# A gated linear attention block and a SiLU feed-forward block on one core: output and state products moved next to the scores of the following chunk

## The chip, the cores and the metric

The kernel runs on one core of one Trainium2 chip. The metric is the device time of one execution in microseconds. The median of three executions of the kernel before is 556.96 us (556.51 to 557.35).

## The reference

The first block is a recurrent linear attention with a gate for each row of the state (4 batches, 8 heads, 768 tokens, head width 48). The second multiplies the 3072 rows of its output by `w_in` (384 x 2048), applies `h * sigmoid(h)`, and multiplies by `w_out` (2048 x 384). q, k, v and alpha are float32, the weights arrive as float64.

```python
for t in range(S):
    state = alpha[:, :, t, :, None] * state + einsum('bhd,bhe->bhde', k[:, :, t], v[:, :, t])
    y[:, :, t] = einsum('bhd,bhde->bhe', q[:, :, t], state)
x = y.transpose(0, 2, 1, 3).reshape(B * S, H * D)
h = x @ w_in
g = h * (1.0 / (1.0 + np.exp(-h)))
return g @ w_out
```

## The kernel before

**Chunks and steps.** The sequence is cut into six chunks of 128 tokens; with four batches this makes NT = 24 chunks of work, n = 0 to 23, where n and n + 4 belong to the same batch. An outer loop over `step` has four quarters (called slots in the code). In each quarter it issues one or two attention stages, and then `fill` issues pieces of the feed-forward block. The stages of chunk n are:

- `products(n)`, in step n, quarter 1: VectorE brings alpha into a transposed layout (32 x 32 block transposes), takes a backward running product of it (a scan, u), the smallest values (`least`), transposes k and forms kp = k * u.
- `quotient(n)`, step n, quarter 2: VectorE takes a reciprocal and a forward scan p, transposes q, and writes p = q * p. The first matmul of the scores waits for this last write.
- `flip(n)`, step n, quarter 3: VectorE transposes kp and a DMA carries it out and back (`land`) to get it in the layout that the states need (kn).
- `scores(n)`, step n + 1, quarter 0: 16 small matmuls of kp and p into two PSUM tiles named ps_a; ScalarE copies them to g, GpSimd masks them; ScalarE scales the state of the batch.
- `values(n)` gives y: 16 matmuls of g with v and 12 of the state with p into a ps_a tile, which ScalarE copies to xt, the input of the feed-forward block. `states(n)` then makes 16 matmuls of kn and v into one more ps_a tile, and VectorE adds them to the state (two additions, `st`). Both stand in step n + 1, quarter 3. From chunk 20 on there is no states stage.

There are three ps_a buffers of one PSUM bank each. Chunks 0 to 7 (NA = 8) use TensorE transposes in place of VectorE's, and `settle` after them frees the memory of the weight conversion and loads the first chunk of the second kind.

**The feed-forward block.** Four chunks make a group (GB = 4, six groups). Groups 0 and 1 use plain products with `w_in` (`enter_plain`): a piece is six matmuls of 128 x 256. Groups 2 to 5 use a fast matrix multiplication with 20 products in place of more (`enter`, seven pieces for each pair of column blocks). It needs sums of blocks of `w_in` (`sums_w`, 23 for each pair, 128 x 256 each, on VectorE) and sums of blocks of x (`sums_x`, 11 for a group, named xc). The product with `w_out` is a Strassen-like scheme (`leave`, seven pieces for each half of a group; a piece is eight matmuls of 128 x 192 into one of two PSUM banks named ps_o). Pieces 1, 3 and 4 of a `leave` end with two subtractions each on cells of g (`subtract`, in place; a subtraction has to wait until TensorE has read those cells), pieces 3, 5, 6 and 7 end with a store of a 128 x 192 block to the output. `side_by_side` is an addition of two cells of g that follows the SiLU of the last piece.

**Order.** `fill` paces the pieces: `marks` gives, for each phase of pieces, the quarter by which it has to be done, and a piece that needs y of a chunk is not issued before `values` of that chunk (`bridged`). From chunk 8 on, TensorE's instructions stay in program order; VectorE's, ScalarE's and the queues' are put in order by the compiler's scheduler where a line does not call `keep_in_program_order`. On the chip each engine works its list off in that order, so an instruction that waits holds up all that stand behind it on its engine. `audit` adds reductions over the inputs on VectorE that decide at the end whether the fast path was valid (a flag, read before the last pieces).

Around step 10 the order of TensorE's work in the kernel before is as follows (P a piece of `enter_plain`, L.k piece k of `leave(0, 1)`, y and S values and states, sc scores):

```text
sc8  P P P  y8 S8  L.1  sc9  P L.2  P L.3  y9 S9  P  sc10  L.4  P L.5  P  y10 S10  L.6  sc11  P L.7  P P  y11 S11
```

Of the kernel before, what the change touches and what calls it, by code (L numbers as in the profile page):

```python
# [13 lines left out]
ALU = mybir.AluOpType  # L14
# [341 lines left out]
def quotients(  # L356
# [20 lines left out]
    dve, act, gps = nc.vector, nc.scalar, nc.gpsimd  # L377
# [17 lines left out]
    C = 128  # L395
# [39 lines left out]
    def ps_attn(n=C):  # L435
        return ps_a.tile([128, 512], F32, name="ps_a").rearrange("p (j c) -> p j c", c=n)
# [152 lines left out]
    def sums_w(pair, upto):  # L589

        r = slice(2 * pair, 2 * pair + 2)
        while sums_done[pair] < min(upto, len(SUMS_W)):
            to, sa, a, sb, b = SUMS_W[sums_done[pair]]
            tc.keep_in_program_order(
                combine(block_w(to)[:, r], sa, block_w(a)[:, r], sb, block_w(b)[:, r]))
            sums_done[pair] += 1
# [108 lines left out]

    def turned(x, to):
        x = x[:, 32:].rearrange("p (g j d) -> p g j d", j=4, d=D)
        dve.transpose(to.rearrange("p g (b j) -> p g j b", j=4), x[:, :, :, 0:32])

    def products(n):  # L710

        c = ctxs[n]
        sg = seg[0 if late else n % 2]
        ps = {}

        for name in ("a", "k", "q"):
            if n >= NA:
                if name == "a":
                    turned(c[name], tokens(sg))
                    load(n + 1, "a")  # L720
                continue
            if n < GB and name != "a":

                at = "kq".index(name)
                ps[name] = (bank(at) if n == 1 else out_bank(at, 512)).rearrange("p (j c) -> p j c", c=C)
            else:
                ps[name] = ps_attn()
            for j in range(NP):
                pe.transpose(ps[name][:, j, :], c[name][:, 2 * j : 2 * j + 2, :], ident)
            if name == "a":  # L730
                act.copy(tokens(sg), ps[name])  # L731
        end = NP * W
        u = upool.tile([128, end + 1], F32, name="u")
        dve.tensor_tensor_scan(u[:, end - 1 :: -1], sg[:, end:0:-1], one[:, end:0:-1],  # L734
                               0.0, ALU.mult, ALU.add)

        dve.tensor_single_scalar(least[:, n, :], u[:, 0:end:W], 2.0**-64, ALU.max)
        kp = c["kp"] = turns(kps, n) if n < NA else kps[0]
        ut = tokens(u)
        if n >= NA:  # L740
            ps["k"] = late["turn"].tile([128, NP, C], F32, name="turn")
            turned(c["k"], ps["k"])
            load(n + 1, "k")
        if n < NA:
            dve.tensor_tensor(kp, ps["k"], ut, ALU.mult)
            quotient(n, sg, ps["q"])
            return
        j = NP // 2
        dve.tensor_tensor(kp[:, 0:j], ps["k"][:, 0:j], ut[:, 0:j], ALU.mult)
        k, ut = [x[:, j:].rearrange("p j (e c) -> p j e c", e=2) for x in (ps["k"], ut)]  # L750
        dve.tensor_tensor(kp[:, j:].rearrange("p j (e c) -> p j e c", e=2)[:, :, ::-1], k, ut, ALU.mult)
        c["sg"] = sg
# [90 lines left out]
    def values(n):  # L843
# [17 lines left out]
        if e == 0:  # L861
            xts[half] = xtp.tile([128, NKT, TB], F32, name="xt")
        act.copy(xts[half][:, :, e * C : (e + 1) * C], py[:, 0:NKT])  # L863
    def states(n):
        c = ctxs.pop(n)
        ci, b, vn = c["ci"], c["b"], c["v"]
        if ci < NCH - 1:

            ps = ps_attn()
            for j in range(NP):  # L870
                for i in range(4):
                    r = slice(32 * i, 32 * i + 32)
                    kn = c["kn"][:, j, r] if n < NA else c["kn"][:, i, 32 * j : 32 * j + 32]
                    pe.matmul(ps[r, j, 0:D], lhsT=kn, rhs=vn[:, 2 * j + i // 2, 0:D],
                              start=True, stop=True)
            for u in range(2):
                r = slice(64 * u, 64 * u + D)
                s, x = st[b][r, :, u, :], ps[r, :, 0:D]
                if ci > 0:
                    dve.tensor_tensor(s, x, s, ALU.add)  # L880
                else:
                    act.copy(s, x)
# [28 lines left out]
    def enter_plain(grp, h, pair):  # L911

        if h == 0:
            g_tiles(grp, pair)
        xt = xts[2 * grp + h]
        for f in range(8 * pair, 8 * pair + 8, 2):
            ps = bank(f // 2 % 3).rearrange("p (e n) -> p e n", e=2)
            for e in range(2):
                for t in range(NKT):
                    pe.matmul(ps[:, e, :], lhsT=w_in[:, t, (f + e) * 128 : (f + e + 1) * 128],  # L920
                              rhs=xt[:, t, :], start=(t == 0), stop=(t == NKT - 1))
            q, i = divmod(f, 4)
            act.activation(gts[grp, h, pair][:, i : i + 2, q % 2, :], ps, AF.Silu)  # L923
            if grp == 1 and pair == h == 0:
                differences(f // 2)
                differences(4 + f // 2)
            if grp > 0 and f % 8 == 6:
                side_by_side(grp, h, pair)
            yield

    def enter(grp, pair):
# [92 lines left out]
    def cells(grp, h, pair, m, k):  # L1024

        return gts[grp, h, pair][:, k::2, :, m * C : (m + 1) * C]
# [3 lines left out]
    def side_by_side(grp, h, pair):  # L1030

        x = cells(grp, h, pair, 1, 0)
        dve.tensor_tensor(x, x, cells(grp, h, pair, 1, 1), ALU.add)

    def leave(grp, h):

# [26 lines left out]

        def done():
            if 2 * grp + h in (1, 2):
                sums_w(2 * grp + h - 1, 4 * next(steps) + 4)

        def new(i):
            return out_bank(i, HO)
# [54 lines left out]
    def group(grp):  # L1124
        return [[(enter(grp, pair), 12, GB * grp + GB)] * 7 for pair in range(2)]

    def output(grp):
        return [[(leave(grp, h), 12, GB * grp + GB)] * 7 for h in range(2)]

    def both(x, y):  # L1130
        for i in range(max(len(x), len(y))):
# [3 lines left out]
    for h in range(2):  # L1135
        for pair in range(2):
            pieces += [plain(0, h, pair)] * 4
    pieces += [plain(1, 0, 0)] * 4 + [(leave(0, 0), 12, GB)] * 7
    phases = [len(pieces)]
    pieces += [plain(1, 1, 0)] * 4  # L1140
    both([(leave(0, 1), 12, GB)] * 7, [plain(1, 0, 1)] * 4 + [plain(1, 1, 1)] * 4)
    phases.append(len(pieces))
    before = output(1)
    for grp in range(2, NG):
# [12 lines left out]

    def go_on():

        nonlocal done  # L1160
        next(pieces[done][0], None)
        done += 1

    audits = audit()
    done, bridged = 0, 0
    STEPS = NT + 1
    SLOTS = 4

    marks = [2 * SLOTS + 2] + [(GB * i + 2 * GB) * SLOTS + 3 for i in range(len(phases))]

    def settle():

        first.close()
        late.update(look=pool("look"), part=pool("part"), turn=pool("turn"),
                    xc=pool("xc").tile([128, len(SUMS_X), TB], F32, name="xc"),
                    wx=pool("wx").tile([128, 8, NQ, 128], F32, name="wx"))
        quads = pool("quads")
        late["p"] = pool("p").tile([128, NP * W + 1], F32, name="p")
        late["quads"] = {name: quads.tile([128, 32 + 4 * NP * D], F32, name=f"{name}t") for name in "akq"}
        for name, t in late["quads"].items():  # L1180
            gps.memset(t, 1.0 if name == "a" else 0.0)
        load(NA)

    def fill(step, slot):

# [16 lines left out]

    for step in range(STEPS):
        if step == 1:
            load(NIN)
        stages = [[(scores, 1)], [(products, 0)], [(values, 1)], [(states, 1)]]
        if step == 1:

            stages = stages[1::-1] + stages[2:]
        elif step >= NA:  # L1210
            stages = [[(land, 1), (scores, 1)], [(products, 0)], [(quotient, 0)],
                      [(values, 1), (states, 1), (flip, 0)]]
        for slot, group in enumerate(stages):
            for stage, lag in group:
                n = step - lag
                if not 0 <= n < NT:
                    continue
                stage(n)
                if stage is values:
                    bridged = n + 1  # L1220
                if stage is states and n + 1 + NIN < NA:
                    load(n + 1 + NIN)
                if stage is states and n + NV < NT:
                    load_v(n + NV)
            if step * SLOTS + slot == (NA + 1) * SLOTS - 1:
                x = decayed.rearrange("p (o i c) -> p o i c", o=2, c=C)
                for r, o in later:
                    gps.memset(x[r, o, :, 0:CH], 0.0)
            fill(step, slot)
            if step * SLOTS + slot >= NA * SLOTS - 1 and conv_done[1] == NFT and not late:  # L1230
                settle()
# [82 lines left out]
```

## Time and profile before

| | |
|---|---|
| median of three executions | 556.96 us |
| the profiled execution | 557.26 us, of which the span from the first to the last instruction is 555.5 us |
| granted TensorE clock | 0.999 |
| TensorE matmul busy (PE) | 541.4 us, 97% of the span |
| weight loads busy (PEld) | 489.7 us, 88% |
| VectorE busy (DVE) | 445.4 us, 80% |
| ScalarE busy (ACT) | 208.5 us, 38% |
| GpSimd busy (POOL) | 76.1 us, 14% |
| DMA | 70.09 MB, mean 126 GB/s |

PE is TensorE's matmuls, PEld its weight loads, DVE VectorE, ACT ScalarE, POOL GpSimd, SPq the DMA queue of SyncE. An fp32 matmul appears as two instructions in the trace, so that a piece of six matmuls shows as x12 and a piece of eight as x16. The end of a matmul is modelled; where exact times matter, starts are compared. In a timeline row the first number is the start in us, the second the time that the row covers, and the bracket at the end gives the idle time before it and what ended it. In the view of waits, the numbers are the us in total, how many times, and the longest.

### The profile page before, as it was taken

The page shows a single profiled execution, that of the slowest core. Times are in us where ns is not written, and L with a number is a line of the kernel's source. Part 1 is how long each engine was busy: PE and PEld are TensorE (multiplying, and loading weights), DVE is VectorE, ACT ScalarE, POOL GpSimd, SP SyncE. Part 2 cuts the span into 40 slices and gives each one's busy share as a digit, 9 for nine tenths or more (in the row PEclk, how much of TensorE's full clock was granted, in tenths as well). Part 3 has the DMA queues.
Part 4 walks back from the last instruction along what each step waited for, and adds up shares of the span by engine and source line. Part 5 has one row for each costly group of instructions (what it writes and reads, how often), then busy time and mean ns, then how long its engine had stood idle before and what let it go on. Part 6 is the DMA issues. An engine that isn't in the chain of part 4 may idle for free. (4 is left out here: it accounts for less than half of the span.)

```text
span 555.5 us, 12640 instructions
## 1 busy us (share of the span) xinstructions
PE 541.4 (97%) x5026; PEld 489.7 (88%) x5026; DVE 445.4 (80%) x801; ACT 208.5 (38%) x466; POOL 76.1 (14%) x146
## 2 busy tenths in 40 slices
PE   6999999999999999999999999999999999999996
PEld 4788887998899999899999999988998999999996
DVE  5897788974999899997998986998884796945431
ACT  2556653223333253353353353344263342332100
POOL 3210000222210212021011021021121000001000
PEclk9999999999999999999999999999999999999999
DMA  9998971164454625355545654617642135500000
GB/s 215 246 249 210 232 195 33 47 161 116 117 136 125 159 63 138 86 145 149 139 112 139 193 139 120 191 27 183 170 137 91 54 91 169 172 11 22 10 24 30
DMA packets 99217, 70.09 MB, mean 126 GB/s; under 512 B 56272, under 2 KB 88656, under 8 KB 99152
## 3 DMA queue, kind: packets, MB, share of 16 engines
q1 hardware_dynamic: 97232, 65.30, 45.1%
q0 software_dynamic: 1920, 3.93, 2.0%
q8 instruction: 40, 0.66, 0.5%
q14 instruction: 25, 0.20, 0.1%
HBM read 61.34 MB, written 7.86 MB: 125 GB/s over the span
## 5 line engine op out<-in xcount | busy, mean ns | idle before, releaser
L388 PE MATMUL ps_o<-w_out,g 128*128 128x192 f32 x768 | 134.0, 328 | 0.5 <-DVE o L1056 0.5
L388 PEld LDWEIGHTS ps_o<-w_out,g 128*128 128x128 f32 x768 | 125.6, 190 | 3.5 <-DVE o L1056 1.0
L388 PE MATMUL ps_m<-xt,w_in 128*128 128x256 f32 x480 | 113.6, 383 | 1.5 <-ACT xt L863 1.1
L388 PEld LDWEIGHTS ps_m<-xt,w_in 128*128 128x128 f32 x480 | 89.1, 190 | 14.4 <-ACT xt L863 1.6
L388 PE MATMUL ps_o<-wt,g 128*128 128x192 f32 x576 | 99.7, 326 | 0.0
L388 PEld LDWEIGHTS ps_o<-wt,g 128*128 128x128 f32 x576 | 95.1, 190 | 1.6 <-issue 0.2
L388 PE MATMUL ps_m<-xc,w_in 128*128 128x256 f32 x288 | 70.7, 382 | 0.0
L388 PEld LDWEIGHTS ps_m<-xc,w_in 128*128 128x128 f32 x288 | 53.7, 190 | 7.0 <-DVE g L958 0.3
L1047 DVE TENSOR_TENSOR g<-g 128x512 f32<-128x512 f32 x72 | 50.1, 709 | 8.3 <-PE ps_o L388 8.3
L955 ACT ACTIVATE g<-g 128x1024 f32<-128x1024 f32 x32 | 33.1, 1056 | 61.2 <-DVE g L958 61.1
L1059 POOL DMA_DIRECT2D out_dram<-o x40 | 22.0, 551 | 219.5 <-DVE o L1056 113.7
L825 POOL TENSOR_SCALAR_AFFINE_SELECT g<-g 64x256 f32<-64x256 f32 x64 | 34.9, 546 | 124.4 <-ACT g L818 105.7
L388 PE MATMUL ps_m<-xc,wx 128*128 128x256 f32 x192 | 50.1, 383 | 1.0 <-DVE xc L586 1.0
L950 ACT COPY g<-ps_m 128x512 f32<-128x512 f32 x64 | 36.6, 588 | 37.0 <-PE ps_m L388 36.9
L388 PEld LDWEIGHTS ps_m<-xc,wx 128*128 128x128 f32 x192 | 35.2, 190 | 5.2 <-ACT u L1078 1.2
L958 DVE TENSOR_TENSOR g<-ps_m,g 128x512 f32<-128x512 f32 x56 | 37.1, 683 | 3.2 <-PE ps_m L388 2.7
L734 DVE TENSOR_TENSOR_SCAN u<-al,one 128x516 f32<-128x516 f32 x24 | 29.8, 1240 | 11.9 <-ACT al L731 11.6
L923 ACT ACTIVATE g<-ps_m 128x512 f32<-128x512 f32 x32 | 19.1, 597 | 41.7 <-PE ps_m L388 41.4
L950 ACT COPY part<-ps_m 128x512 f32<-128x512 f32 x32 | 18.9, 590 | 38.0 <-PE ps_m L388 24.0
L697 DVE TENSOR_REDUCE seen<-bits 128x1 f32<-128x512 int32 (+1 forms) x33 | 26.3, 823 | 5.7 <-DMA bits<-in_moe_w_in_dram 5.7
L764 DVE TENSOR_TENSOR_SCAN p<-al,inv 128x516 f32<-128x516 f32 x24 | 29.9, 1247 | 1.0 <-PE ps_a L388 0.3
L1056 DVE TENSOR_TENSOR o<-ps_o,u 128x192 f32<-128x192 f32 x24 | 8.5, 355 | 25.7 <-PE ps_o L388 22.8
(129 smaller groups left out, 648.5 us busy)
## 6 DMA issues: line engine op xcount, KB each, us to landing
bits<-in_moe_w_in_dram SPq DMA_DIRECT2D x24, 512.0 KB, 4.7
bits<-in_moe_w_out_dram SPq DMA_DIRECT2D x16, 384.0 KB, 3.9
at<-in_alpha_dram SPq DMA_DIRECT2D x64, 96.0 KB, 2.5
kt<-in_k_dram SPq DMA_DIRECT2D x64, 96.0 KB, 2.6
qt<-in_q_dram SPq DMA_DIRECT2D x64, 96.0 KB, 2.7
bits<-in_alpha_dram SPq DMA_DIRECT2D x9, 512.0 KB, 4.0
out_dram<-o POOLq DMA_DIRECT2D x40, 96.0 KB, 2.4
flips<-turn SPq DMA_DIRECT2D x12, 256.0 KB, 2.4
```

The source lines that it names most:

```text
L388: in_order(nc.tensor.matmul(*args, **kw))
L697: dve.tensor_reduce(seen[kind][which][:, i : i + 1], x, axis=AX, op=op, apply_absolute_value=True))
L734: dve.tensor_tensor_scan(u[:, end - 1 :: -1], sg[:, end:0:-1], one[:, end:0:-1], 0.0, ALU.mult, ALU.add)
L764: dve.tensor_tensor_scan(p[:, 0:end], sg[:, 0:end], iv[:, 0:end], 0.0, ALU.mult, ALU.add)
L825: gps.affine_select(x, x, pattern=[[0, NP], [1, CH]], compare_op=ALU.is_ge, fill=0.0, base=0, channel_multiplier=-1)
L923: act.activation(gts[grp, h, pair][:, i : i + 2, q % 2, :], ps, AF.Silu)
L950: act.copy(to, ps)
L955: act.activation(x, x, AF.Silu)
L958: dve.tensor_tensor(to, a, b, op)
L1047: dve.tensor_tensor(cells(grp, h, pair, *to), cells(grp, h, pair, *x), cells(grp, h, pair, *y), ALU.subtract)
L1056: dve.tensor_tensor(o, x, y, ALU.add)
L1059: (gps if grp < NG - 1 else nc.sync).dma_start(out[r : r + C, c * HO : (c + 1) * HO], o)
```

## The change

Seven edits, all of them in where work is issued; the number of matmuls, of VectorE operations and of bytes stays the same.

1. From step 9 on (chunks 8 to 23), `values(n)` and `states(n)` move from step n + 1, quarter 3, to step n + 2, quarter 0, directly ahead of `scores(n + 1)`. One more step is run (STEPS = NT + 2).
2. `states` then writes into a ps_o bank that the running `leave` does not hold at that moment (`left` counts its pieces) and no longer into a ps_a tile. When the next `leave` piece is the second or the fifth, that piece is issued first.
3. The end of each phase of pieces but the first is two quarters later (`marks`).
4. In `enter_plain` of group 1, the `side_by_side` addition is issued one piece later (`owed`).
5. Eight of the 23 sums of `w_in` for pair 0 are issued with the four pieces of `plain(1, 1, 0)`, and eight for pair 1 with the last two pieces of `leave(0, 1)`; both were issued later.
6. `settle` loads alpha of chunk 8 first, then v, then k and q; v of chunk 8 was loaded before in the quarter after `states(6)`.
7. A few instructions are pinned to program order (the first k transposes of chunk 9, an addition of g).

```diff
-            turned(c["k"], ps["k"])
+            turn_k = turned(c["k"], ps["k"])
+            if n == NA + 1:
+                tc.keep_in_program_order(turn_k)
...
-    def states(n):
+    def states(n, behind=False):
...
-            ps = ps_attn()
+            if behind:
+                ps = out_bank(0 if left in (3, 4, 5) else 1, 512).rearrange("p (j c) -> p j c", c=C)
+            else:
+                ps = ps_attn()
...
+            if grp == h == 1 and pair == 0:
+                sums_w(0, f + 2)
             if grp > 0 and f % 8 == 6:
-                side_by_side(grp, h, pair)
+                owed.append((done, grp, h, pair))
...
-        dve.tensor_tensor(x, x, cells(grp, h, pair, 1, 1), ALU.add)
+        add = dve.tensor_tensor(x, x, cells(grp, h, pair, 1, 1), ALU.add)
+        if grp == h == 1:
+            tc.keep_in_program_order(add)
...
         def done():
             if 2 * grp + h in (1, 2):
-                sums_w(2 * grp + h - 1, 4 * next(steps) + 4)
+                n = 4 * next(steps) + 4
+                sums_w(2 * grp + h - 1, n)
+                if grp == 0:
+                    sums_w(1, n - 20)
...
-        nonlocal done
+        nonlocal done, left
+        if pieces[done][0] in leaves:
+            left = left % 7 + 1
         next(pieces[done][0], None)
+        while owed and owed[0][0] < done:
+            side_by_side(*owed.pop(0)[1:])
         done += 1
...
-    STEPS = NT + 1
+    STEPS = NT + 2
...
-    marks = [2 * SLOTS + 2] + [(GB * i + 2 * GB) * SLOTS + 3 for i in range(len(phases))]
+    marks = [2 * SLOTS + 2] + [(GB * i + 2 * GB) * SLOTS + 3 + 2 * (i > 0) for i in range(len(phases))]
...
-        load(NA)
+        load(NA, "a")
+        load_v(NA)
+        load(NA, "kq")
...
-            stages = [[(land, 1), (scores, 1)], [(products, 0)], [(quotient, 0)],
-                      [(values, 1), (states, 1), (flip, 0)]]
+            lag = 2 if step > NA else 1
+            y = [(values, lag), (states, lag)]
+            stages = [[(land, 1), (scores, 1)], [(products, 0)], [(quotient, 0)], [(flip, 0)]]
+            stages[0 if lag == 2 else 3][0:0] = y
...
+                if stage is values and lag == 2 and left in (1, 4) and pieces[done][0] in leaves:
+                    go_on()
-                stage(n)
+                if stage is states:
+                    states(n, lag == 2)
+                else:
+                    stage(n)
...
-                if stage is states and n + NV < NT:
+                if stage is states and n + NV < NT and n + NV != NA:
                     load_v(n + NV)
```

Around step 10 TensorE's work in the changed kernel stands in this order:

```text
sc8  P P P  L.1  y8 S8 sc9  P L.2  P L.3  y9 S9 sc10  P L.4  P L.5  y10 S10 sc11  P L.6  P L.7  y11 S11 sc12
```

## The prediction

> **What bounds the kernel now.** I read the page first, then the view of waits of TensorE, then the timeline around each wait, and last the order in which VectorE's instructions stand in the built programs.
>
> ```profile
> PE 541.4 (97%) x5026; PEld 489.7 (88%) x5026; DVE 445.4 (80%) x801; ACT 208.5 (38%) x466; POOL 76.1 (14%) x146
> ...
> DVE  5897788974999899997998986998884796945431
> ```
>
> PE is busy all the time, so a microsecond in which it waits is a microsecond of the total; VectorE is nearly full in the middle slices too. What is left to gain is in PE's waits from step 10 on:
>
> ```profile
> PE ps_m L388 <- DVE xc L586: 1.0, 1, 1.0
> ...
> PE ps_a L388 <- DVE p L770: 0.5, 1, 0.5
> PE ps_m L388 <- DVE g L958: 0.4, 1, 0.4
> ```
>
> By the starts of matmuls these three cost 2.5 us: 1.13 at 367.1, 0.64 at 143.0 and 0.72 around 228. A fourth of that size, for the store `o` at 531.5, lies in the tail and stays.
>
> The third view is what a score block waits for. These are the timelines of TensorE and of VectorE around y of chunk 10 (columns: start, us, engine, line, operation):
>
> ```profile
> 168.76 2.75 PE L388 MATMUL ps_m<-xt,w_in 128*128 128x256 f32 x12
> 171.44 1.08 PE L388 MATMUL ps_a<-g,vn 128*32 128x128 f32 x32
> 172.34 0.84 PE L388 MATMUL ps_a<-p,st 128*32 128x128 f32 x24
> 173.00 0.52 PE L388 MATMUL ps_a<-vn,kn 128*32 128x48 f32 x32
> 173.45 2.87 PE L388 MATMUL ps_o<-w_out,g 128*128 128x192 f32 x16
> 176.25 0.90 PE L388 MATMUL ps_a<-p,kp 48*64 48x128 f32 x32
> ```
>
> ```profile
> 169.57 0.35 DVE L1056 TENSOR_TENSOR o<-ps_o,u 128x192 f32<-128x192 f32 x1
> 169.84 0.41 DVE L587 SCALAR_TENSOR_TENSOR w_in<-wx,w_in 128x256 f32<-128x256 f32 x1
> 170.17 0.88 DVE L582 TENSOR_TENSOR w_in<-wx,w_in 128x256 f32<-128x256 f32 x2
> 170.97 0.42 DVE L584 TENSOR_TENSOR w_in<-w_in 128x256 f32<-128x256 f32 x1
> 171.30 1.22 DVE L708 STREAM_TRANSPOSE turn<-kt 128x512 f32<-128x512 f32 x1
> 172.56 0.43 DVE L749 TENSOR_TENSOR kp<-turn,u 128x256 f32<-128x256 f32 x1
> 172.90 0.42 DVE L751 TENSOR_TENSOR kp<-turn,u 128x256 f32<-128x256 f32 x1
> 173.36 1.11 DVE L708 STREAM_TRANSPOSE turn<-qt 128x512 f32<-128x512 f32 x1
> 174.50 0.69 DVE L770 TENSOR_TENSOR p<-turn,p 128x512 f32<-128x512 f32 x1
> ```
>
> The store `o` empties the bank of L.5, which PE left at 168.76. The k and q transposes and p of chunk 11 stand behind it on VectorE's list, 5.6 us from 169.57 to 175.19. PE does not notice: between L.5 and the scores at 176.25 it has a plain piece (2.7 to the next start), y and states (171.44 to 173.45, 2.0) and L.6 (2.8).
>
> **The change part by part.** The sum is made against the profiled execution, 557.26 us, which stands 0.3 us above the median of 556.96.
>
> *Visits to the small matmuls.* y, states and scores are one visit in place of two, 15 times (y of chunks 8 to 22). What a visit costs PE besides its matmuls: the first piece behind it takes 0.11 longer (2.87 for the x16 at 173.45, 2.76 for the one at 518.64 below); on the way in, the last wide matmul starts 0.31 before the first small one (159.72 to 160.03) where wide ones follow each other by 0.22, 0.09 more; and the first wide one after the states starts some 0.11 late. A merged visit saves at most these 0.31, and nothing if the turn from states to scores costs as much. The nearest row, a score block that follows states directly at 17.77, starts 0.21 behind the last of them; I take 0.16, 15 x 0.16 = 2.4 us, ends 0 and 4.6. [...]
>
> *Scores of steps 10 to 13.* Here the change costs. With four pieces in a step in place of five, a `leave` piece now stands directly ahead of y, and the scores directly behind the states. From the end of that piece to the scores PE has 0.1 + 2.0 = 2.1 us of work. VectorE's list in the changed program keeps the subtraction or the store of that very piece in front of the k transpose:
>
> ```text
> step 10 (chunk  9): sub(L.1) kt kp kp w w qt sub(L.1) p
> step 11 (chunk 10): sub(L.3) kt sub(L.3) kp kp w qt w p
> step 12 (chunk 11): o(L.5) w w w w kt kp kp qt p
> step 13 (chunk 12): o(L.7) w w kt w kp kp w qt xc p
> ```
>
> (sub a subtraction of 512 columns, w a sum of w_in.) As steps between starts in the timeline: sub 0.60, kt 1.06, the two kp 0.80, qt 1.05, w 0.34, o 0.27, p whole 0.69. A subtraction starts when PE has read half the piece:
>
> ```profile
> 518.64 2.76 PE L388 MATMUL ps_o<-w_out,g 128*128 128x192 f32 x16
> ...
> 520.14 0.69 DVE L1047 TENSOR_TENSOR g<-g 128x512 f32<-128x512 f32 x1 [0.61 <-PE ps_o L388]
> ```
>
> 1.5 us after its start, with PE's way to the scores then 2.6 + 2.1 = 4.7. Step 10: 1.5 + 5.5 - 4.7 = 2.3 us of wait. Step 11: 1.5 + 5.6 - 4.7 = 2.4. Step 12: the rows above give the same ten operations as 5.6; with 0.2 from PE's end to the store, 5.8 - 2.1 = 3.7, and by the steps between starts 3.4; I take 3.5. Step 13: two more small sums and one store step instead of the longer sum, 5.7 + 0.2 - 2.1 = 3.8. Together 12.0, where before there were 0.6. VectorE is idle ahead of each of these pieces (about 8 us of work per step against PE's 11), so each wait starts anew and they add; ends 10 and 14. Deferring `side_by_side` does remove VectorE's 7.6 us wait for a SiLU, but the subtraction of L.1 then waits at the same place, to 139.9 where the sum was at 139.21.
>
> *Later steps.* With seven pieces in a step, the scores have cover. What is late next is xc, whose last nine sums now come behind the group's last two products. For group 4 VectorE has, from the product before them to the xc sum that the second entry piece reads, 37 operations: 14 x 0.60, 8 sums 2.9, alpha's chain 3.9, two transposes 2.1, two kp 0.8, two reductions 1.2, two stores 0.6, state additions 0.7, together 20.6. PE has 1.7 + 2.1 + 1.0 + 2.6 + 1.7 + 2.6 + 2.6 + 2.6 = 16.9. Wait 3.8; the same count before gives 1.2 where the trace shows 1.13. Likewise groups 3 and 5 give 0.7 and 0.3, and the first piece of `leave(3, 1)`, whose bank is emptied behind the chain of chunk 23, 1.5. Together 6.3; I take 6, ends 2 and 8. The 2.5 us of before are replaced by these.
>
> *What costs nothing, and why.* States in the ps_o bank wait for its store: ScalarE's copy after L.3 ends 0.4 after PE, VectorE's after L.5 1.0 in this phase and 2.7 at most, ahead of 2.0 us of y; uncovered it costs 0.7 once. L.2 reuses the bank of states 8: the state additions that free it end 2.7 after p on VectorE's list, PE has the scores and a plain piece of 3.6 in that time; without it, up to 2.7. v's loads go out a quarter later, behind flip on SP's queue and waiting there for the states, with kn and the next alpha behind them; all are used a step or two on, 14 us or more against the 2.7 that q's loads take to land. Alpha first at `settle` only reorders SP. The masks on POOL, with the output stores behind them, get a quarter more; ScalarE's copies of y and scores come in a row of 3 us, and the plain pieces have three banks. The 16 earlier sums (0.34 each) fill VectorE's idle stretch after 131.6 or stand in the lists above; without that they cost 5.4.
>
> Sum: 557.3 - 2.4 + 12.0 + 6 - 2.5 = 570.4 in the profile, 570 as a median.
>
> **The rivals.**
>
> *Only the scores wait.* The late xc is worked off while VectorE gains from PE's four waits. For it: VectorE at 250 to 260 has 31% free. Against: the waits of group 4 start from a place 170 us later. 557.3 - 2.4 + 12.0 + 0.5 - 2.5 = 564.9, median 564.6.
>
> *Faster.* One mechanism: VectorE reaches the k transposes before the `leave` piece ends, so that p is ready when the states are. Then the saved visits and the removed waits stand: 557.3 - 2.4 - 2.5 = 552.4. For it: kt of chunk 9 is fetched at 121 and transposed at 139.8, so the data would be there. Against: VectorE runs its list in order, and 5.6 us of it hang on a piece that ends 2.1 us ahead of the scores. It decides if all new waits together stay under 4.9 us.
>
> *No change.* Waits near 4.9 us, which needs the lists above to be wrong by half.
>
> **How the numbers follow.** Scores and later waits 0.72 (566 to 575); only the scores 0.16 (562 to 566); faster 0.07; no change 0.02; more than 575 by waits that I did not count 0.03. Predicted 570. All low costs together with the largest saving give 557.3 - 4.6 + 10 + 2 - 2.5 = 562.2, all high ones 576.8; the range is 562 to 575, which leaves about 1 in 8 out. About 0.2% is what a measurement of this kernel can tell from no change. Slower 0.72 + 0.16 + 0.03 = 0.91, same 0.02, faster 0.07.
>
> **What would show it.** PE's waits would have ps_a waiting for p four times or more, 10 us or more in total, at the first four merged visits after 140 us, each with VectorE idle shortly before, waiting for ps_o. xc would have 3 us or more near group 4's entry. The pieces behind merged visits would be as long as behind single ones, and 15 fewer. Wrong is it if p waits stay under 3 us in total: then VectorE's list is not what holds the scores.

## The result and the profile after

The changed kernel takes 581.17 us (median of five executions, 579.68 to 582.60) against 557.35 for the kernel before: a ratio of 1.0429 (95% interval 1.0413 to 1.0446), 4.3% slower. The profiled execution is the shortest of the five, 579.68 us with a span of 578.0, against 557.26 and 555.5. The forecast was 570, slower, with a range of 562 to 575: the sign and the place were right, the size was not.

The page of the changed kernel: the line of busy times, and three rows of the 40 equal slices.

```profile
PE 546.1 (94%) x5026; PEld 495.3 (86%) x5026; DVE 446.3 (77%) x801; ACT 209.3 (36%) x466; POOL 83.1 (14%) x146
...
PE   6999999998987799999999999989979999999995
DVE  5897889985877789997899997998874576974431
...
PEclk9999999999987999999999999999999999999998
```

The row of PE has its dips in slices 10 to 14 (130 to 202 us, steps 10 to 13) and again in slices 27 and 30. The third row, the granted clock, was all nines in the kernel before:

```profile
PEclk9999999999999999999999999999999999999999
```

Here it falls to 8 and 7 in the middle of the first group of dips. PE's busy time went up by 4.7 us although it has the same 5026 instructions: some of them ran slower.

The view of TensorE's waits (us in total, how many, the longest):

```profile
PE ps_a L388 <- DVE p L772: 11.1, 4, 3.6
PE ps_o L388 <- DVE o L1065: 5.2, 3, 3.4
...
PE ps_m L388 <- DVE xc L586: 2.0, 2, 1.8
```

The first row is what was forecast: four waits of ps_a for p, at the scores of chunks 9 to 12. The other two belong to later stages. This is the third of them, chunk 11, on TensorE:

```profile
171.08 2.76 PE L388 MATMUL ps_o<-w_out,g 128*128 128x192 f32 x16
173.78 1.08 PE L388 MATMUL ps_a<-g,vn 128*32 128x128 f32 x32
174.67 0.84 PE L388 MATMUL ps_a<-p,st 128*32 128x128 f32 x24
175.33 0.52 PE L388 MATMUL ps_o<-vn,kn 128*32 128x48 f32 x32
179.48 1.56 PE L388 MATMUL ps_a<-p,kp 48*64 48x128 f32 x32 [3.62 <-DVE p L772]
180.97 5.21 PE L388 MATMUL ps_m<-xt,w_in 128*128 128x256 f32 x12
```

and on VectorE:

```profile
173.88 0.36 DVE L1065 TENSOR_TENSOR o<-ps_o,u 128x192 f32<-128x192 f32 x1 [1.28 <-PE ps_o L388]
174.16 0.42 DVE L587 SCALAR_TENSOR_TENSOR w_in<-wx,w_in 128x256 f32<-128x256 f32 x1
174.49 0.88 DVE L582 TENSOR_TENSOR w_in<-wx,w_in 128x256 f32<-128x256 f32 x2
175.29 0.42 DVE L584 TENSOR_TENSOR w_in<-w_in 128x256 f32<-128x256 f32 x1
175.62 1.07 DVE L708 STREAM_TRANSPOSE turn<-kt 128x512 f32<-128x512 f32 x1
...
178.64 0.69 DVE L772 TENSOR_TENSOR p<-turn,p 128x512 f32<-128x512 f32 x1
```

VectorE stands idle for 1.28 us until TensorE has finished the `leave` piece, does the store `o` and the four sums, and only then takes up the k transpose, whose input was fetched from 157.2 on and landed 2.6 us after issue at the latest; p is done at 179.33 and the scores start at 179.48. Two rows of TensorE's view show what I did not forecast: the scores take 1.56 us where they otherwise take 0.90, and the plain piece behind them 5.21 where the x12 in the forecast's rows took 2.75. Both ran at half speed: the granted clock is 0.50 to 0.51 from 178.9 to 185.7 us.

By the starts of matmuls, from the same point at 116 us on, the last matmul starts 21.3 us later than before. It divides as follows:

| Part | us |
|---|---|
| waits for p at the scores of chunks 9 to 12: 2.27, 2.03, 3.69, 3.43 | +11.4 |
| matmuls at half rate behind three of these waits | +6.3 |
| waits from chunk 13 on (xc, `o` and others), the tail's 0.67 included | +9.5 |
| waits of the kernel before: 0.64, 0.72, 1.20, and the tail's 0.67 (1.20 is the prediction's 1.13 with the 0.07 by which the first matmul behind the wait is longer) | -3.2 |
| 15 merged visits of 0.196 each | -2.9 |
| not assigned | +0.2 |

The span grew by 1.1 us more behind VectorE's last instruction, where only the last output and the program's end lie. What causes that is not shown.

### The profile page after: what moved, and what is told of

It is laid out like the page before. It is cut to its first block, busy times and chain, and to the rows that moved or that the text cites. A ratio compares the mean times of both kernels' runs of the same rounds, so it can differ in the third digit from the quotient of the medians.

```text
span 578.0 us, 12629 instructions
## 1 busy us (share of the span) xinstructions
PE 546.1 (94%) x5026; PEld 495.3 (86%) x5026; DVE 446.3 (77%) x801; ACT 209.3 (36%) x466; POOL 83.1 (14%) x146
## 5 line engine op out<-in xcount | busy, mean ns | idle before, releaser
L388 PE MATMUL ps_m<-xt,w_in 128*128 128x256 f32 x480 | 118.6, 395 | 1.1 <-ACT xt L865 1.1
L388 PEld LDWEIGHTS ps_m<-xt,w_in 128*128 128x128 f32 x480 | 92.7, 197 | 15.3 <-ACT xt L865 1.6
L1056 DVE TENSOR_TENSOR g<-g 128x512 f32<-128x512 f32 x72 | 48.3, 683 | 20.2 <-PE ps_o L388 20.2
L827 POOL TENSOR_SCALAR_AFFINE_SELECT g<-g 64x256 f32<-64x256 f32 x64 | 40.9, 640 | 75.1 <-ACT g L820 60.6
L388 PE MATMUL ps_a<-p,kp 48*64 48x64 f32 (+2 forms) x640 | 26.3, 273 | 11.1 <-DVE p L772 11.1
L388 PEld LDWEIGHTS ps_a<-p,kp 48*64 48x64 f32 (+1 forms) x640 | 22.2, 157 | 15.3 <-issue 14.0
```

The costliest lines, as they stand in the source:

```text
L388: in_order(nc.tensor.matmul(*args, **kw))
L827: gps.affine_select(x, x, pattern=[[0, NP], [1, CH]], compare_op=ALU.is_ge, fill=0.0, base=0, channel_multiplier=-1)
L1056: dve.tensor_tensor(cells(grp, h, pair, *to), cells(grp, h, pair, *x), cells(grp, h, pair, *y), ALU.subtract)
```

## Experiments

All are made from the changed kernel unless it says otherwise. Each ratio is against executions of the kernel before on the same chip.

| Kernel | median, us | ratio to before (95% interval) |
|---|---|---|
| changed kernel | 581.17 | 1.0429 (1.0413 to 1.0446) |
| move undone | 561.50 | 1.0075 (1.0058 to 1.0092) |
| VectorE's order mended | 563.75 | 1.0125 (1.0096 to 1.0153) |
| waits filled with matmuls | 571.95 | 1.0263 (1.0242 to 1.0285) |
| phase ends undone | 581.85 | 1.0436 (1.0416 to 1.0456) |
| move and phase ends undone | 556.67 | 0.9988 (0.9976 to 1.0000) |
| ten chunks moved | 557.59 | 1.0008 (0.9998 to 1.0018) |
| nine chunks moved, reductions later | 555.58 | 0.9975 (0.9964 to 0.9986) |
| no move, reductions later | 557.80 | 1.0011 (1.0001 to 1.0022) |

### The move undone

```diff
-            lag = 2 if step > NA else 1
+            lag = 1
...
-            stages = [[(land, 1), (scores, 1)], [(products, 0)], [(quotient, 0)], [(flip, 0)]]
-            stages[0 if lag == 2 else 3][0:0] = y
+            stages = [[(land, 1), (scores, 1)], [(products, 0)], [(quotient, 0)], y + [(flip, 0)]]
```

> Only edits 1 and 2 are undone: y and states stand in quarter 3 again, with a ps_a tile for states; the later phase ends, the early sums of w_in, the late addition of g and the load order stay as in the changed kernel (578.0 us span). Theory A (the 11.4 us of score waits come from VectorE's list when a leave piece and y directly precede the scores, and the half-rate stretches of TensorE come from these waits): no wait of ps_a for p above 0.7 us, granted clock 0.999, the 15 visits are separate again (+2.9 us), some of the later waits for o and xc stay because the phase ends do (2 to 4 us in total): span 557 to 561. Rival B (the later phase ends or the early sums fill VectorE so that p is late wherever y stands): waits for p stay at 5 us or more and the span is above 565.

It took 561.50 us, the profiled span is 559.7 and the granted clock 0.997. TensorE's waits, of those after 115 us that are above 1 us or wait for p:

```profile
PE ps_o L388 <- DVE o L1065: 3.4, 4, 1.4
PE ps_o L388 <- ACT g L962: 1.3, 1, 1.3
...
PE ps_a L388 <- DVE p L772: 0.3, 1, 0.3
```

Of the 11.1 us for p, 0.3 are left. The rows for `o` and g stay: they belong to the later phase ends, since the run without these (edits 4 to 7 alone) has 0.8 for `o` and none for g. With the other edits in place, the move makes the difference of 19.7 us to the changed kernel; the other edits together cost 4 us without it. Rival B is out.

### VectorE's order mended

For chunks 9 to 12 the transposes and p are tied to the order in which the program issues them, and with them the subtractions and stores of `leave(0, 1)`; the move stays.

```diff
-            if n == NA + 1:
+            if NA < n <= NA + 4:
                 tc.keep_in_program_order(turn_k)
...
-            turned(c["q"], q)
+            turn_q = turned(c["q"], q)
+            if NA < n <= NA + 4:
+                tc.keep_in_program_order(turn_q)
...
-        dve.tensor_tensor(qp, q, qp, ALU.mult)
+        mul_q = dve.tensor_tensor(qp, q, qp, ALU.mult)
+        if NA < n <= NA + 4:
+            tc.keep_in_program_order(mul_q)
...
-            if behind:
+            if behind and n != 10:
...
+                if grp == 0 and h == 1:
+                    tc.keep_in_program_order(ins)
```

The last two added lines stand behind each subtraction of `subtract` and behind the addition in `store`, whose instruction is named `ins`.

> The changed kernel with y and states where it puts them, but for chunks 9 to 12 the k and q transposes and p, and the subtractions and stores of leave(0, 1), keep program order on VectorE, so that the transposes stand ahead of the subtraction or store of the piece before y; states of chunk 10 use a ps_a tile. Theory A: the waits of ps_a for p go from 11.1 us to under 1, the clock goes to 0.999, the later waits for o and xc (7.2 us) stay or shrink a little: 578.0 - 11.4 - 6.5 = 560, span 558 to 563. Rival B (a merged visit is slow by itself, or the half rate comes from the denser order of work and not from waits): the waits move to another place of the same steps or the clock stays under 0.99; span 568 or more.

It took 563.75 us, span 561.4. On VectorE p of chunk 11 now stands ahead of the store instead of behind it:

```profile
168.79 0.69 DVE L774 TENSOR_TENSOR p<-turn,p 128x512 f32<-128x512 f32 x1
169.51 0.71 DVE L786 STREAM_TRANSPOSE turn<-kp 128x512 f32<-128x512 f32 x1
170.15 0.32 DVE L1071 TENSOR_TENSOR o<-ps_o,u 128x192 f32<-128x192 f32 x1
```

By the starts, 0.7 and 1.25 us of the waits for p are left, at chunks 11 and 12, together twice the "under 1" of theory A. Behind the first of them the scores take 0.90 us and the next piece 2.86, and the granted clock is 1.00 from 19 us to the end of the work (the mean of 0.994 holds one half-rate stretch of 3.4 us in the start, before anything that the change touches). The waits of the later stages stay, 9.7 us against 9.5. So the order of VectorE's instructions in four steps, with the bank of states 10, is worth 17.4 us of the median, and a merged visit is not slow by itself.

### The waits filled

```diff
+        for _ in range({9: 9, 10: 8, 11: 15, 12: 14}.get(n, 0)):
+            pe.matmul(ps[0][:, 0, :], lhsT=ident, rhs=ident, start=True, stop=True)
         for j in (0, 2, 1, 3):
```

This stands in `scores(n)`. It adds work that is of no use and leaves VectorE's order alone.

> The changed kernel with 9, 8, 15 and 14 additional matmuls of 128 x 128 ahead of the scores of chunks 9, 10, 11 and 12, whose results the scores overwrite; at the rate of the other 128-column matmuls (0.214 us each) they fill 1.9, 1.7, 3.2 and 3.0 us of the waits of 2.3, 2.0, 3.7 and 3.4, and leave VectorE's lists alone. Theory A (the half rate follows from TensorE standing idle): the granted clock stays 0.998 or more away from the end, the waits left are under 0.7 each, and the span falls by the 6.5 us of slow matmuls to 571.5 (570 to 573), although 9.8 us of work are added. Rival B (the half rate comes with the order of the work or with its power): the clock keeps its dips after 157 us and the span stays 577 to 580; if the work added costs time as such, more.

It took 571.95 us, 9.2 less than the changed kernel with 46 matmuls more; the profiled span is 570.4. Chunk 11 on TensorE:

```profile
173.55 0.52 PE L388 MATMUL ps_o<-vn,kn 128*32 128x48 f32 x32
174.00 3.62 PE L388 MATMUL ps_a<-ident 128*128 128x128 f32 x30
177.54 0.90 PE L388 MATMUL ps_a<-p,kp 48*64 48x128 f32 x32
178.38 2.86 PE L388 MATMUL ps_m<-xt,w_in 128*128 128x256 f32 x12
```

The scores still start 4.0 us behind the states, now behind 3.6 us of filling, but they take 0.90 and the next piece 2.86. The filling takes 0.24 us for each matmul, 11.0 in all, somewhat more than the 9.8 that I had counted, and in the profiled execution no stretch at half rate is left before the end of the work at 568 us (of the three others two have a mean clock of 0.997, one of 0.989). The rate therefore followed TensorE's standing still here, not the order of its work. Of the 7.6 us by which the span is shorter, 6.3 are the half rate; the later waits came out 0.6 shorter, the filling is 0.4 shorter than the waits that it stands for, the end is 0.1 shorter, and 0.2 are not assigned.

### The phase ends undone

```diff
-    marks = [2 * SLOTS + 2] + [(GB * i + 2 * GB) * SLOTS + 3 + 2 * (i > 0) for i in range(len(phases))]
+    marks = [2 * SLOTS + 2] + [(GB * i + 2 * GB) * SLOTS + 3 for i in range(len(phases))]
```

> Only edit 3 is undone: each phase of pieces ends two quarters earlier again, so that five pieces stand in most of the steps 10 to 13. Theory A with my reading that four pieces in a step put a leave piece directly ahead of y: the waits for p of the four chunks fall from 11.1 us to about 3 (2 and 1.3 at chunks 9 and 11), the clock dips go or become one, but xc of groups 3 and 4 is then late, 5 to 7 us each, against 0.2 and 2.0: all waits after 115 us are 18 to 22 us against 19 to 21, and the span is 570 to 580. Rival B (the pace of the pieces has no part in the waits for p): they stay at 10 us or more.

It took 581.85 us, no other than the changed kernel, but by another way (span 581.2, waits and the entry of group 4):

```profile
PE ps_m L388 <- DVE xc L586: 12.4, 2, 6.9
...
PE ps_a L388 <- DVE p L772: 4.1, 3, 2.2
```

```profile
379.90 2.76 PE L388 MATMUL ps_o<-wt,g 128*128 128x192 f32 x16
389.54 2.05 PE L388 MATMUL ps_m<-xc,wx 128*128 128x256 f32 x4 [6.88 <-DVE xc L586]
```

With five pieces in a step the waits for p fall to 4.1 us, which is the direction that I had read from the order, though not the 3 expected; chunk 9 still waits 2.27. xc of groups 3 and 4 is late by 5.6 and 7.0 us, and the matmuls behind both waits run at half rate (2.05 for x4, which is 1.03 otherwise), as do those behind the wait of chunk 9. So there are three dips of the clock where I expected one or none, the waits come to some 23 us by the starts against 18 to 22, and the span lies above the 580 of theory A. Without the later phase ends, the moved y makes the sums of x late; with them, the scores' cover is gone. Seen with the move undone, the later phase ends cost by themselves: 561.50 against 556.67 in the next run.

### Edits 4 to 7 alone

The edits of the first and the fourth experiment together.

> Edits 1, 2 and 3 are undone; the late addition of g, the early sums of w_in, the load order and the pins stay. Theory A (all the lost time comes with the move and with the later phase ends, and the sums fill idle stretches of VectorE): span 555.5 less up to 1, since the addition of g no longer holds VectorE for 7.6 us before the scores of chunk 9; waits of TensorE as before or smaller, none above 1.2 us. Rival B (the sums or the late addition cost time of their own): span 557.5 or more, with a wait above 1.5 us that the kernel before does not have.

556.67 us, a ratio of 0.9988; the profiled span is 553.8, 1.7 less than before where theory A had up to 1. That execution is one of the faster ones: the median is only 0.3 below the kernel before, and the interval reaches 1.0000. The wait before the scores of chunk 9 (0.64) is gone, and the 0.72 around 228 is 0.31. So the early sums of w_in and the late addition cost nothing that can be measured, and all of the loss lies in the move and the phase ends.

### Part of the move

Two kernels move y and states for a part of the chunks only, with the order of the second experiment for chunks 9 to 12 and phase ends one quarter later.

```diff
-            lag = 2 if step > NA else 1
-            y = [(values, lag), (states, lag)]
+            def together(n):
+                return 9 < n < NT - 1 and n % GB != 3
             stages = [[(land, 1), (scores, 1)], [(products, 0)], [(quotient, 0)], [(flip, 0)]]
-            stages[0 if lag == 2 else 3][0:0] = y
+            if together(step - 2):
+                stages[0][0:0] = [(values, 2), (states, 2)]
+            if not together(step - 1):
+                stages[3][0:0] = [(values, 1), (states, 1)]
...
-    marks = [2 * SLOTS + 2] + [(GB * i + 2 * GB) * SLOTS + 3 + 2 * (i > 0) for i in range(len(phases))]
+    marks = [2 * SLOTS + 2] + [(GB * i + 2 * GB) * SLOTS + 3 + (i > 0) for i in range(len(phases))]
```

> The changed kernel, but y and states are moved to the next scores only for ten chunks (10, 12, 13, 14, 16, 17, 18, 20, 21, 22): not for the last chunk of a group, whose y the following group waits for, and not for chunks 8 and 9; the later phases end one quarter later instead of two; and VectorE keeps k and q transposes and p ahead of the subtractions and stores of leave(0, 1) for chunks 9 to 12. Theory A: a merged visit saves 0.196 us of TensorE, 2.0 in all; the waits for p stay under 0.5 us, xc of group 4 about 1.1, no half rate: span 553 to 554.5, 0.2 to 0.5% faster than before. Rival B (merging gives no gain that the waits of the later stages do not take back): span 555.5 or more.

557.59 us, a ratio of 1.0008: no gain; the span of 555.1 lies between the 554.5 of theory A and the 555.5 of rival B. The ten visits are 0.196 shorter each, and xc takes 1.5 us in two waits, but a wait stands where I had none:

```profile
210.47 1.13 PE L388 MATMUL ps_m<-xc,wx 128*128 128x256 f32 x4
211.44 1.89 PE L388 MATMUL ps_m<-xc,w_in 128*128 128x256 f32 x8
214.78 1.54 PE L388 MATMUL ps_o<-w_out,g 128*128 128x192 f32 x8 [1.45 <-DVE st L889]
```

The `leave` piece waits for the state additions (`st`) to free the ps_o bank that the states were put into. Edit 2 costs that much here.

In the second of the two, `together` begins at chunk 12, and the reductions of steps 17 to 19 go to the end:

```diff
-        if at % 2 == 0 and step > 3 * GB + 2:
+        if at % 2 == 0 and step > 3 * GB + 2 and step not in (17, 18, 19):
```

> As the kernel with ten chunks moved, without chunk 10, and the reductions of steps 17 to 19 over the inputs are issued at the end instead, so that xc of group 4 has VectorE for itself. Theory A: 1.8 us from merged visits and 0.9 from the wait for xc at group 4's entry, of which up to 0.8 comes back behind the reductions at the end: span 552.5 to 554.5. Rival B: xc waits as before (1.1 us), or the reductions delay the tail by more than 1 us: span 555 or more.

555.58 us, a ratio of 0.9975 (0.9964 to 0.9986): 0.25% faster than before, the one version whose interval lies wholly below 1, and 1.1 us less than edits 4 to 7 alone. The profiled execution, with a span of 552.9, is the shortest of twelve. The waits for p and xc are gone from the view, and what is left by the starts after 130 us is 0.3, 0.5, the tail's 0.67 and two of 0.2.

The same reductions with no move and the old phase ends:

> Edits 1, 2 and 3 are undone as in the run of edits 4 to 7 alone, and the reductions of steps 17 to 19 are issued at the end. It differs from the kernel with nine chunks moved by the move, its pins and the phase ends. Theory A: slower than that one by the nine merged visits, 1.8 us less the waits that the move brings: 1 to 2 us, span 554 to 555.5. Rival B: equal or faster, so that merged visits are worth nothing here.

557.80 us, 2.2 more than with nine chunks moved, which theory A had at 1 to 2; the span of 556.2 lies above its 555.5. But the waits differ too, not only the visits: xc at group 4 takes 1.45 us here, with a reduction of 1.21 us that was not moved still among its sums, and `leave` has 0.80 at 477. So this comparison does not isolate the value of a merged visit; the traces do, below. That pausing these reductions alone would cure xc was wrong.

## Why the prediction was wrong

*Scores of steps 10 to 13: right.* Predicted 2.3, 2.4, 3.5, 3.8, together 12.0; measured 2.27, 2.03, 3.69, 3.43, together 11.4, in these places, each with VectorE idle ahead of it for TensorE. The undone move takes these waits away (0.3 left in the view) and the mended order most of them (1.8 left), by two different ways. The reading that a fifth piece in a step would have covered them is borne out in the main: 4.1 us in place of 11.1. The lists of steps 10 and 11 hold the same operations, so that the 5.6 us taken for the second should have been 5.5, which changes nothing.

*What failed: the sum has no term for the rate of matmuls behind a wait.* I counted each wait of TensorE as its own length and added the four up, and worked with the trace of before, where the granted clock is 1.00 to the end of the work and no wait from step 10 on is longer than 1.13 us; there the case does not occur. In the changed kernel three of the four waits are followed by stretches at half rate, 6.3 us more. This term alone would have put the sum at 576.7, above the range; the later waits alone, at 573.2, would not. The view by windows of the changed kernel, in stretches of 3.4 us laid on the grid of its half-rate periods (columns: window, length, then busy us and count of PE, PEld, DVE, ACT, POOL, granted clock, share of DMA, GB/s):

```profile
141.40:144.80 3.40, 1.64 (x80) 1.50 (x72) 3.37 (x8) 0.51 (x2) 0.00 (x0) 1.00 0.30 70
158.50:161.90 3.40, 1.44 (x55) 1.23 (x43) 3.39 (x8) 0.63 (x2) 0.00 (x0) 1.00 0.79 198
161.90:165.30 3.40, 3.40 (x10) 2.65 (x9) 3.25 (x6) 2.35 (x10) 2.46 (x4) 0.50 0.59 164
...
175.50:178.90 3.40, 0.35 (x35) 0.22 (x21) 3.30 (x6) 0.48 (x1) 0.00 (x0) 1.00 0.37 101
178.90:182.30 3.40, 2.82 (x35) 2.54 (x36) 3.29 (x6) 1.12 (x5) 0.36 (x1) 0.51 0.84 241
182.30:185.70 3.40, 3.40 (x9) 2.68 (x9) 2.44 (x4) 1.43 (x6) 3.03 (x4) 0.50 0.57 122
...
417.90:421.30 3.40, 1.53 (x8) 1.00 (x6) 3.33 (x6) 1.83 (x8) 2.11 (x4) 1.00 0.63 204
421.30:424.70 3.40, 1.82 (x11) 1.83 (x12) 2.94 (x7) 1.25 (x2) 0.56 (x1) 1.00 0.38 55
```

In this view the clock in a window answers to the window ahead of it. With 1.64 us of work in it (the wait of chunk 9), the next is full; with 1.44 (chunk 10) the next is at 0.50; with 0.35 (chunk 11) the next two are, the first of which begins within the wait and holds 2.82. The window of chunk 12, 196.0 to 199.4, holds 0.07, and the next is at 0.50. The longest wait of the later stages, 3.45 us of idle time from 419.4, lies across two windows with 1.53 and 1.82 and costs no rate. What a wait cost beyond itself thus depended on how it fell on this grid. The kernel with the phase ends undone shows it on a wait of the same length: chunk 9 waits 2.27 us there too, but the window holds 1.20, and the next is at half rate:

```profile
142.10:145.50 3.40, 1.20 (x64) 1.09 (x57) 3.40 (x8) 0.48 (x1) 0.00 (x0) 1.00 0.46 117
145.50:148.90 3.40, 3.40 (x37) 2.91 (x38) 3.34 (x7) 1.67 (x8) 0.82 (x2) 0.50 0.80 217
```

The four other executions of the changed kernel have a mean granted clock of 0.980 or 0.981 against 0.986, and are 1.2 to 2.9 us longer; where the grid lies in them is not shown.

The length of a wait alone did not decide it: the one of 2.03 us among small matmuls (chunk 10) is followed by half rate, those of 2.27 (chunk 9) and 3.45 are not.

*Later steps: mis-sized.* I took 6 us; measured are 8.8 without the tail's wait. Two of my four places were right in kind and wrong in size: group 4's entry had 3.8 and measured 2.0, and TensorE came to it later, having lost 2.0 us before and within the first piece of `leave(3, 0)`, which I had not counted; that this made the rest of the difference is not shown by a run. (20.6 - 16.9 is 3.7, not 3.8.) The first piece of `leave(3, 1)`, with 1.5 in the forecast, waits 3.6 by the starts:

```profile
419.56 1.08 DVE L708 STREAM_TRANSPOSE turn<-qt 128x512 f32<-128x512 f32 x1
420.68 0.69 DVE L772 TENSOR_TENSOR p<-turn,p 128x512 f32<-128x512 f32 x1
421.28 1.27 DVE L697 TENSOR_REDUCE seen<-bits 128x1 f32<-128x512 int32 x2
422.47 0.35 DVE L1065 TENSOR_TENSOR o<-ps_o,u 128x192 f32<-128x192 f32 x1
```

The store that empties its bank stands behind the chain of chunk 23, as I said, but also behind q's transpose, p and two reductions. Groups 3 and 5, with 0.7 and 0.3, had 0.2 and 0.5.

*Merged visits: 0.16 taken, 0.196 measured.* Before, y with states took 2.584 us from the last wide matmul's start to the second one behind, and the scores 1.406; merged they take 3.415. Each of these counts one wide step on either side. A merged visit needs these two steps only once, and their plain time is 0.379 (0.217 for a matmul of 256 columns, 0.162 for one of 192), so 2.584 + 1.406 - 3.415 - 0.379 = 0.196, and 0.197 in the visits without states. The states take 0.45 from their start to the next matmul, whether that is a score or a wide one: the turn to the scores costs nothing beyond that. 15 x 0.196 = 2.9 us, against the 2.4 in the sum.

*The 2.5 us of before* are gone, as taken. Of *what costs nothing*, one item shows a price in a neighbour of the change: the state additions that free the ps_o bank were covered in the changed kernel, and cost 1.6 us by the starts with ten chunks moved, inside the 2.7 that I had named as its bound.

Put in the prediction's sum, by spans: 568.6 forecast, + 6.3 half rate, + 2.8 later waits, - 0.6 scores, - 0.5 visits, + 1.1 behind the last VectorE instruction, + 0.2 not assigned = 577.9, where 578.0 was measured. The range missed it because it ended at 575, below even the 576.8 of all high ends together, and left no room for a term that I did not have.

## What to carry to other kernels

Before a stage is moved next to another, look at what the engine that feeds the second has on its list in between: here the order of some ten VectorE instructions in each of four steps decided 17 us, and the merged visits were worth 2.9 by the starts. Price a forecast wait on TensorE with what comes behind it: more than about 2 us in which it does little was followed here, by the position of a window, by nothing or by 3.4 or 6.8 us at half rate. A stage whose result others wait for is better left in place: the moved y made xc late by 5.6 and 7.0 us where the phases ended early, and the states in a ps_o bank held up a `leave` piece by 1.6.

## What the runs showed of the hardware

The half rate came here in windows of 3.4 us on a grid, and followed the busy time of the window ahead. In the changed kernel it goes from 161.9 to 165.3, from 178.9 to 185.7 and from 199.4 to 202.8 us, one or two windows long, with the starts five and six windows apart. In the profiled executions of the kernel before, the changed kernel and the first four experiments, each window of 3.4 us at full rate that holds one of the longer waits after 115 us, and 1.44 us of modelled TensorE time or less, is followed by one at half rate (1.44, 1.20, 0.61, 0.35 among them), and each with 1.53 or more (1.53, 1.59, 1.60, 1.61, 1.64, 1.67 and above) by one at full rate. The line lies between, for these stages. It is no general threshold: in the start of the kernel with the mended order the window from 12.2 to 15.6 us holds 1.6 us of other matmuls, and the next is at half rate. Useless matmuls held the rate here: 11.0 us of them made the kernel 9.2 us shorter.
